# Hash-masked attention and a gated feed-forward block on one core: all engines in source order, a first pair prepared head by head, five pairs transposed on TensorE

## The chip, the cores and the metric

The kernel runs on one core of a Trainium2 chip. The core has TensorE (PE in the profile, with its weight loads as PEld), VectorE (DVE), ScalarE (ACT), GpSimd (POOL) and SyncE (SP, which here only issues DMAs), and 16 DMA engines that all queues share. The metric is the device time of one execution, in microseconds. Three runs of the kernel before took 406.2, 409.23 and 409.6 us; the median is 409.23.

## The reference

There are 4 batches, 8 heads, 768 tokens and a head size of 64. Each token of q and k is hashed to six bits, and a query sees only the keys with the same six bits. The result goes, as 3072 tokens of 512 features, through a feed-forward block with a gelu gate and a sigmoid-gated residual.

```python
q_bits = einsum('bhsd,dk->bhsk', q, proj) > 0          # six bits for each token
mask = q_bucket[:, :, :, None] == k_bucket[:, :, None, :]
scores = where(mask, q @ k.T / sqrt(D), -1e9)
attn = exp(scores - max) / (sum + 1e-09)
x = (attn @ v)                                          # 3072 x 512
g, val = x @ w_gate, x @ w_val                          # 512 x 1536 each
out = x + sigmoid(x @ w_res) * ((gelu(g) * val) @ w_out)
```

## The kernel before

Work is done by pairs of heads: 16 pairs, four to a batch. For each pair and side (q is side 0, k is side 1) a tile `nat` holds 12 blocks (two heads of six) of 128 tokens, and for each token 64 features, six hash bits as plus or minus a half, and a constant. Transposed, it is `aug`: 71 rows, of which a matmul gives q times k and the number of equal bits in one go, so that an exponential with a large scale leaves only the keys whose six bits all agree. No mask is built.

**Preparation.** `prep` (L156) does this for one or two pairs. GpSimd casts the loaded q and k into `nat` (L138, L140). DVE transposes the float32 loads in blocks of 32 (L168), PE multiplies them by the projection, up to four tiles side by side in 32 columns each (L175), DVE transposes the sums back (L181), and compares make the bits (L186), four for each tile. Then a DMA transpose on SyncE's queue turns `nat` into `aug` (L191). `values_of` (L142) makes bf16 values and sums of values on GpSimd.

**Attention.** A chunk is two PSUM banks of 512 scores; nine chunks make a pair. `scores` (L248) runs the score matmuls (L255) into `sp` (two buffers) and the exponential on ScalarE (L260), then `flush` runs the value matmuls of the chunk before (L235, eight for a chunk) into `av`, which each head starts with one matmul (L228). `finish` (L207) divides (L214, L215) and, after the second head, a DMA transpose makes `x_sb` (L218).

**Feed-forward.** `gate_val(b)` (L266) has 24 groups of eight matmuls (L276) with gelu on ScalarE (L282) and a product on DVE (L283). It needs `x_sb` of all four pairs of its batch. `project(b)` (L287) has for each of six token tiles four matmuls into `rps` (L293), a tanh (L296), 12 matmuls into `fps` (L300), two DVE operations (L305, L307) and the store (L309). It is a generator, cut into 30 pieces of about three matmuls.

**Order.** The main loop (L343) walks groups of two pairs, 18 chunks each. In each slot it emits scores, now and then a load, one step of the next group's `prep`, and from batch 1 on a piece of the last batch's `project`. `gate_val(b-1)` comes after slot 3 (`LEAD = 4`) of batch b, the last one at the end. This is the order of emission: the recording layer then schedules the instructions on each engine by priorities and a model of their durations, so that what is emitted later can stand earlier on an engine. Pools set which buffers must come free: `ld` 3, `ldv` 2, `nat` 4, `aug` 4 for each side, `sp` 2, `av` 2, and two PSUM buffers `mm` that the hash sums, `rps` and `fps` share. The weights are 12 loads from GpSimd's queue (L96), which change float32 to bf16 on the way.

Of the kernel before, what the change touches and what calls it, by code (L numbers as in the profile page):

```python
# [9 lines left out]
FP32 = mybir.dt.float32  # L10
# [7 lines left out]
def kernel(  # L18
# [32 lines left out]


    EPS = 2.0 ** -90

    const = ctx.enter_context(tc.tile_pool(name="const", bufs=1))


    projw = const.tile([P, 2, 32], FP32, name="projw")
    nc.vector.memset(projw, 0.0)
    for a in range(4):  # L60
        nc.scalar.dma_start(projw[32 * a:32 * a + 32, :, NBITS * a:NBITS * (a + 1)],
                            proj.rearrange("(h r) n -> r h n", r=32))
    eps_sb = const.tile([P, P], BF16, name="eps_sb")
    nc.gpsimd.memset(eps_sb, EPS)
    warm = const.tile([P, 512], BF16, name="warm")
    nc.gpsimd.memset(warm, 0.0)

# [3 lines left out]
    for i in range(NN):  # L71
        nat.append(const.tile([P, HT, P], BF16, name=f"nat{i}"))
        eng = nc.vector if i < 2 else nc.gpsimd
        eng.memset(nat[i][:, :, D:P], 0.0)
        eng.memset(nat[i][:, :, D + NBITS:KA], 1.0 if i % 2 == 0 else -NBITS / 4.0)

    w_pool = ctx.enter_context(tc.tile_pool(name="w", bufs=1))
# [16 lines left out]
    def load_w():  # L94
        if wload:
            nc.gpsimd.dma_start(*wload.pop(0))  # L96

    x_pool = ctx.enter_context(tc.tile_pool(name="x", bufs=2))
    hh_pool = ctx.enter_context(tc.tile_pool(name="hh", bufs=1))
    g_pool = ctx.enter_context(tc.tile_pool(name="gtmp", bufs=2))  # L100
    o_pool = ctx.enter_context(tc.tile_pool(name="omoe", bufs=2))
    ld_pool = ctx.enter_context(tc.tile_pool(name="ld", bufs=3))
    ldv_pool = ctx.enter_context(tc.tile_pool(name="ldv", bufs=2))
    aug_pool = ctx.enter_context(tc.tile_pool(name="aug", bufs=4))
    t32_pool = ctx.enter_context(tc.tile_pool(name="t32", bufs=5))
    va_pool = ctx.enter_context(tc.tile_pool(name="va", bufs=4))
    e_pool = ctx.enter_context(tc.tile_pool(name="e", bufs=4))
    sm_pool = ctx.enter_context(tc.tile_pool(name="sm", bufs=2))
    sc_ps = ctx.enter_context(tc.tile_pool(name="sc_ps", bufs=2, space=PSUM))
    av_ps = ctx.enter_context(tc.tile_pool(name="av_ps", bufs=2, space=PSUM))  # L110
    mm_ps = ctx.enter_context(tc.tile_pool(name="mm_ps", bufs=2, space=PSUM))

    raw, rawv, aug, vaug = {}, {}, {}, {}
    x_tok, x_sb = {}, {}

    def load(p):
        b, hp = divmod(p, HP)
        for side, src in ((0, q), (1, k)):
            s = ld_pool.tile([P, HT, D], FP32, tag=f"ld{side}", name=f"ld{side}")
            nc.sync.dma_start(  # L120
                s.rearrange("p (h t) d -> p h (t d)", h=2),
                src[b, 2 * hp:2 * hp + 2].rearrange("h (p t) d -> p h (t d)", t=T))
            raw[p, side] = s
        vs = ldv_pool.tile([P, 2, T, D], FP32, tag="ldv", name="ldv")
        nc.sync.dma_start(
            vs, v[b, 2 * hp:2 * hp + 2].rearrange("h (p t) d -> p h t d", t=T))
        rawv[p] = vs
# [4 lines left out]
    def cast(x, eng):  # L132
        scale = (1.0 / C) if x[1] == 0 else 1.0
        dst = nat_of(x)[:, :, 0:D]
        if eng is nc.scalar:
            nc.scalar.activation(dst, raw[x], AF.Copy, scale=scale)
        elif x[1] == 0:
            eng.tensor_scalar(dst, raw[x], scale, 1.0, op0=ALU.mult, op1=ALU.mult)  # L138
        else:
            eng.tensor_copy(dst, raw[x])  # L140

    def values_of(p):  # L142
# [3 lines left out]
        nc.gpsimd.memset(va[:, :, :, D:D + 1], 1.0)  # L146
        vsum = va_pool.tile([P, 2, D + 2], BF16, tag="vsum", name="vsum")
# [6 lines left out]
        vaug[p] = (va, vsum)  # L154

    def prep(ps, first=False):  # L156

        jobs = [(p, side) for p in ps for side in range(2)]
        n = 32 * len(jobs)
        hs = mm_ps.tile([P, HT, 32], FP32, tag="mm", name="hs")  # L160
        for i, x in enumerate(jobs):
            cast(x, nc.scalar if first and i == 0 else nc.gpsimd)
        yield
        for h in range(2):
            t32 = []
            for x in jobs:
                tt = t32_pool.tile([P, T, 2, 32], FP32, tag="t32", name="t32")
                nc.vector.transpose(tt.rearrange("p c h n -> p (c h n)"),  # L168
                                    raw[x][:, h * T:(h + 1) * T].rearrange("p c d -> p (c d)"))
                t32.append(tt)  # L170
                if len(t32) % 2 == 0:
                    yield
            for dh in range(2):
                for j, tt in enumerate(t32):
                    nc.tensor.matmul(hs[32 * j:32 * j + 32, h * T:(h + 1) * T, :],  # L175
                                     projw[:, dh, :], tt[:, :, dh, :],
                                     start=(dh == 0), stop=(dh == 1),
                                     tile_position=(0, 32 * j))
            yield
        ht = sm_pool.tile([P, HT, 32], FP32, tag="ht", name="ht")  # L180
        nc.vector.transpose(ht[:n].rearrange("p c n -> p (c n)"),  # L181
                            hs[:n].rearrange("p c n -> p (c n)"))
        for j, x in enumerate(jobs):
            del raw[x]
            for a in range(4):
                nc.vector.tensor_scalar(  # L186
                    nat_of(x)[32 * a:32 * a + 32, :, D:D + NBITS],
                    ht[32 * j:32 * j + 32, :, NBITS * a:NBITS * (a + 1)], 0.0, 0.5,
                    op0=ALU.is_gt, op1=ALU.subtract)
            ag = aug_pool.tile([P, HT, P], BF16, tag=f"aug{x[1]}", name=f"aug{x[1]}")  # L190
            nc.sync.dma_start_transpose(out=ag, in_=nat_of(x).rearrange("p c n -> p (c n)"))  # L191
            aug[x] = ag
            yield
        for p in ps:
            values_of(p)
            yield
# [8 lines left out]
    av = {}  # L205

# [41 lines left out]
    def scores(p, c):  # L248
# [12 lines left out]
        flush()  # L261
        pending.append((p, c, e))
# [24 lines left out]
    def project(b):  # L287

        hh = hidden.pop(b)
        for t in range(T):  # L290
            rps = mm_ps.tile([P, DMODEL], FP32, tag="mm", name="rps")
# [3 lines left out]
            th = g_pool.tile([P, DMODEL], FP32, tag="th", name="th")  # L295
            nc.scalar.activation(th, rps, AF.Tanh, scale=0.5)  # L296
            yield
            fps = mm_ps.tile([P, DMODEL], FP32, tag="mm", name="fps")
            for m in range(KF):
                nc.tensor.matmul(fps, hh[:, m, bass.ts(t, P)], wo[:, m, :],  # L300
                                 start=(m == 0), stop=(m == KF - 1))
                if m % 3 == 2 and m < KF - 1:
                    yield
# [8 lines left out]
    wps = mm_ps.tile([P, 512], FP32, tag="mm", name="wps")  # L312
    for i in range(14):
        nc.tensor.matmul(wps, eps_sb, warm, start=True, stop=True)

    def run(gen):
        for _ in gen:
            pass

    load(0)  # L320
    run(prep((0,), first=True))
    load(1)
    load(2)
    run(prep((1,)))
    load(3)

    NG = NPAIR // 2
    LEAD = 4
    HELD = 6
    mlp = []  # L330

    def mlp_piece():
        while mlp:
            g = mlp[0]
            try:
                next(g[0])
                g[1] += 1
                return
            except StopIteration:
                mlp.pop(0)  # L340

    done = object()
    for g in range(NG):  # L343
        b, half = divmod(g, HP // 2)
        side = prep((2 * g + 2, 2 * g + 3)) if g + 1 < NG else iter(())
        for s in range(2 * NCH):
            p, c = 2 * g + s // NCH, s % NCH
            scores(p, c)
            if s == 0 and g + 2 < NG:
                load(2 * g + 4)  # L350
            if s == NCH and g + 2 < NG:
                load(2 * g + 5)
            if s in (3, 6, 9, 12, 15) and g < 3:
                load_w()
            next(side, None)
            if b >= 1:
                slot = half * 2 * NCH + s
                if slot < LEAD:
                    mlp_piece()
                    mlp_piece()  # L360
                elif slot > LEAD and mlp and mlp[0][1] < 5 * T - HELD:
                    mlp_piece()
# [8 lines left out]
    while mlp:  # L371
        mlp_piece()
# [32 lines left out]
```

## Time and profile before

| what | us |
|---|---|
| median of three runs (lowest, highest) | 409.23 (406.2, 409.6) |
| profiled execution, from its first to its last instruction (span) | 404.7 |
| between that span and the three runs' times | 1.5 to 4.9, 4.5 to the median |
| first score matmul | 21.7 |
| first `gate_val` matmul (the four begin at) | 98.2, 182.5, 268.5, 346.5 |
| PE busy | 366.9 |
| ACT busy | 206.9 |
| DVE busy | 170.7 |
| POOL busy | 81.5 |
| DMA time of the hardware queue, of the weight loads (shares 44.7% and 8.7%) | 181, 35 |

The page gives no time of its own for the profiled execution beyond its span, so the times of the runs are set beside it. In the page's second part the span is cut into 40 slices of 10.1 us; a digit is the busy share of a slice in tenths, and the row PEclk gives the clock that TensorE was granted in tenths of full speed. A busy share counts an instruction's whole duration, and matmuls overlap each other, so that 9 doesn't mean that TensorE runs at its peak. In a list of instructions the number in front is the start, the next one the time that the merged group took; what stands in brackets is the idle time of the engine just before it and what ended that.

### The profile page before, as it was taken

The numbers are of one execution on the slowest core, as the hardware profiler recorded it, in microseconds if no ns is written. First come the engines' busy times: TensorE is split into PE (matmuls) and PEld (weight loads), VectorE is DVE, ScalarE is ACT, GpSimd is POOL, SyncE is SP. The second block draws the span as 40 slices with busy tenths as digits, with TensorE's granted clock in tenths as the row PEclk, the third lists the DMA queues.
The fourth block names the chain that finished last, engine by engine and source line by source line (L and its number), as shares of the span: only waits on it lengthen the run. The fifth ranks groups of instructions, "written<-read, shape, count | busy, mean of one in ns | idle before, by whom it ended". The sixth has DMA issues, their size and how long they took to land. (4 is left out here: it accounts for less than half of the span.)

```text
span 404.7 us, 7265 instructions
## 1 busy us (share of the span) xinstructions
PE 366.9 (91%) x2944; PEld 202.2 (50%) x2990; DVE 170.7 (42%) x366; ACT 206.9 (51%) x225; POOL 81.5 (20%) x149
## 2 busy tenths in 40 slices
PE   6386969959999999998999999899999999999995
PEld 2133524425566555554665555556655555565542
DVE  3727123715433324734336537443336232333342
ACT  2036534636332877773335886863357788333210
POOL 7456245344300022241000342310000000000000
PEclk9759555865999999999999999999999999999999
DMA  7999999996910048776000973920008221100012
GB/s 220 223 270 245 159 239 285 201 238 142 238 55 2 28 84 188 137 186 202 2 0 2 185 205 85 185 47 2 0 2 158 76 68 47 45 2 0 16 65 78
DMA packets 86177, 46.61 MB, mean 115 GB/s; under 512 B 64640, under 2 KB 83072, under 8 KB 86144
## 3 DMA queue, kind: packets, MB, share of 16 engines
q1 hardware_dynamic: 79488, 40.91, 44.7%
q0 software_dynamic: 6336, 5.24, 8.7%
q8 instruction: 23, 0.38, 0.4%
q14 instruction: 10, 0.08, 0.1%
q10 hardware_dynamic: 320, 0.01, 0.0%
HBM read 29.37 MB, written 6.29 MB: 88 GB/s over the span
## 5 line engine op out<-in xcount | busy, mean ns | idle before, releaser
L260 ACT ACTIVATE e<-sp 128x1024 bf16<-128x1024 f32 x144 | 144.4, 1022 | 83.8 <-PE sp L255 82.4
L255 PE MATMUL sp<-aug,aug 71*128 71x256 bf16 (+1 forms) x384 | 98.2, 362 | 4.3 <-DMA aug<-nat 4.1
L282 ACT ACTIVATE gt<-sp 128x768 bf16<-128x768 f32 x48 | 38.9, 810 | 83.3 <-PE sp L276 83.3
L283 DVE TENSOR_TENSOR hh<-gt,sp 128x768 bf16<-128x768 bf16 x48 | 45.8, 953 | 81.1 <-PE sp L276 81.1
L235 PEld LDWEIGHTS <-e 128*128 128x128 bf16 x1152 | 54.3, 104 | 43.1 <-ACT e L260 24.0
L276 PE MATMUL sp<-x_sb,wg 128*128 128x512 bf16 (+1 forms) x382 | 72.0, 328 | 2.6 <-DMA x_sb<-x_tok 2.1
L300 PE MATMUL fps<-wo,hh 128*128 128x512 bf16 x265 | 71.4, 379 | 1.7 <-issue 0.5
L276 PE MATMUL sp<-x_sb,wv 128*128 128x512 bf16 (+1 forms) x371 | 70.0, 324 | 1.2 <-DVE hh L283 0.5
L235 PE MATMUL av<-va,e 128*128 128x65 bf16 x1152 | 66.1, 204 | 2.2 <-ACT e L260 1.1
L168 DVE STREAM_TRANSPOSE t<-ld 128x384 f32<-128x384 f32 x64 | 33.8, 557 | 43.8 <-DMA ld<-in_q_dram 21.3
L276 PEld LDWEIGHTS <-wg 128*128 128x128 bf16 x384 | 37.5, 98 | 28.1 <-issue 3.9
L255 PEld LDWEIGHTS <-aug 71*128 71x128 bf16 x384 | 34.8, 105 | 32.4 <-issue 6.5
L276 PEld LDWEIGHTS <-wv 128*128 128x128 bf16 x384 | 37.7, 98 | 25.8 <-issue 1.2
L175 PE MATMUL hs<-t,projw 128*32 128x192 f32 x256 | 27.3, 375 | 17.8 <-DVE t L168 11.7
L300 PEld LDWEIGHTS <-hh 128*128 128x128 bf16 x288 | 24.3, 97 | 24.0 <-issue 5.3
L305 DVE SCALAR_TENSOR_TENSOR o<-th,fps 128x512 f32<-128x512 f32 x24 | 16.4, 683 | 39.4 <-PE fps L300 29.6
L186 DVE TENSOR_SCALAR nat<-ht 32x72 bf16<-32x72 f32 x128 | 31.3, 244 | 2.3
L214 DVE RECIPROCAL rec<-av 128x6 f32<-128x6 f32 x32 | 6.0, 187 | 56.0 <-PE av L235 56.0
L138 POOL TENSOR_SCALAR nat<-ld 128x768 bf16<-128x768 f32 x15 | 12.4, 829 | 73.8 <-DMA aug<-nat 73.8
L296 ACT ACTIVATE th<-rps 128x512 f32<-128x512 f32 x24 | 14.3, 596 | 21.0 <-PE rps L293 17.7
L145 POOL CAST va<-ldv 128x768 bf16<-128x768 f32 x16 | 13.2, 822 | 57.2 <-PE av L235 52.5
L293 PE MATMUL rps<-wr,x_sb 128*128 128x512 bf16 x88 | 24.3, 382 | 0.1
(34 smaller groups left out, 152.9 us busy)
## 6 DMA issues: line engine op xcount, KB each, us to landing
ld<-in_q_dram SPq DMA_DIRECT2D x16, 384.0 KB, 4.7
ld<-in_k_dram SPq DMA_DIRECT2D x16, 384.0 KB, 4.6
ldv<-in_v_dram SPq DMA_DIRECT2D x16, 384.0 KB, 5.0
out_dram<-o SPq DMA_DIRECT2D x24, 256.0 KB, 2.1
wg<-in_moe_w_gate_dram POOLq DMA_DIRECT2D x4, 384.0 KB, 9.6
wv<-in_moe_w_val_dram POOLq DMA_DIRECT2D x4, 384.0 KB, 7.1
wo<-in_moe_w_out_dram POOLq DMA_DIRECT2D x3, 512.0 KB, 10.7
aug<-nat SPq DMA_TRANSPOSE x32, 4.9
```

The source lines that it names most:

```text
L168: nc.vector.transpose(tt.rearrange("p c h n -> p (c h n)"), raw[x][:, h * T:(h + 1) * T].rearrange("p c d -> p (c d)"))
L175: nc.tensor.matmul(hs[32 * j:32 * j + 32, h * T:(h + 1) * T, :], projw[:, dh, :], tt[:, :, dh, :], start=(dh == 0), stop=(dh == 1), tile_p ...
L186: nc.vector.tensor_scalar(nat_of(x)[32 * a:32 * a + 32, :, D:D + NBITS], ht[32 * j:32 * j + 32, :, NBITS * a:NBITS * (a + 1)], 0.0, 0.5, o ...
L235: nc.tensor.matmul(av[p, hi][:, qt, :], e[:, off:off + P], va[:, hi, jt, 0:D + 1], start=False, stop=(jt == T - 1), skip_group_check=True)
L255: nc.tensor.matmul(sp[:, off:off + nq * P], ks[0:KA, hi * T + jt, :], qs[0:KA, hi * T + qt0:hi * T + qt0 + nq, :], start=True, stop=True)
L260: nc.scalar.activation(e, sp, AF.Exp, scale=float(ALPHA))
L276: nc.tensor.matmul(sp[:, c0:c1], w[:, kk, bass.ts(m, P)], xs[:, kk, c0:c1], start=(kk == 0), stop=(kk == KM - 1))
L282: nc.scalar.activation(gt, sp[:, 0:S], AF.Gelu)
L283: nc.vector.tensor_mul(hh[:, m, :], gt, ps[1][:, 0:S])
L293: nc.tensor.matmul(rps, x_sb[b][:, kk, t, :], wr[:, kk, :], start=(kk == 0), stop=(kk == KM - 1))
L300: nc.tensor.matmul(fps, hh[:, m, bass.ts(t, P)], wo[:, m, :], start=(m == 0), stop=(m == KF - 1))
L305: nc.vector.scalar_tensor_tensor(o, th, 1.0, fps, op0=ALU.add, op1=ALU.mult)
```

## The change

All pools are opened at the top and the whole body is put under a manual schedule: every engine runs its instructions in the order of the source. The main loop is written out for this.

- **Start.** Pair 0 is loaded head by head, q from SyncE's and k from ScalarE's queue. The projection is loaded once (`projn`, 32 rows) and copied by GpSimd into two layouts. Six TensorE fills of 512 columns and six of 256 replace 14 of 512. Head 0 of pair 0 is hashed, turned on TensorE (`turn_pe`) and copied out of PSUM (`turned`, one on ScalarE, one on DVE); head 1 follows in slots 1 and 2.
- **Pairs 1 to 4** are hashed two tiles at a time, a quarter in each slot, and turned on TensorE in groups of six blocks (24 a pair), which DVE copies into `aug`. Pairs 5 to 15 keep the DMA transpose. The bits of k go to GpSimd.
- **Lag.** A chunk's value matmuls come two chunks after its scores (`LAG = 2`), so `LEAD` is 5 and `gate_val(b-1)` stands after slot 4.
- **Project** yields after each matmul; in each slot as many are taken as keep 96 even over 36 slots.
- **Buffers.** `ld` 4, `ldv` 3, `t32` 4 of twice the size; PSUM `mm` becomes one buffer `r` (hash sums, `rps`, q's transposes) and one buffer `f` (`fps`, k's transposes).
- **Casts.** In `prepare`, the line with the cast stands behind the loop over the tiles, so that of each call's tiles only the last is cast: of the 22 casts of pairs 5 to 15, 6 are made. For the other tiles the feature columns of `nat` keep those of an earlier pair. This part of the computation is left out.

The core of the diff:

```diff
+    ctx.enter_context(tc.manual_schedule())
...
+    load_head(0, 0, 0, nc.sync)
+    load_head(0, 1, 0, nc.scalar)
+    projn = const.tile([32, 2, NBITS], FP32, name="projn")
+    nc.sync.dma_start(projn, proj.rearrange("(h r) n -> r h n", r=32))
...
+    def turn_pe(p, side, hi):
...
+        pt = mm_ps.tile([P, T, P], BF16, tag="f" if side else "r", name="pt")
+        for t in range(T):
+            nc.tensor.transpose(pt[0:KA, t, :], nat_of(x)[:, hi * T + t, 0:KA], ident)
+        pts[p, side, hi] = pt
...
+    fill(6)
+    spread(lambda a: projs[32 * a:32 * a + 32, :, 32 * a:32 * a + NBITS], nc.gpsimd)
+    for side in range(2):
+        tr(0, side, 0, 1)
+        cast(0, side, nc.scalar if side == 0 else nc.gpsimd, 0, 1)
+    for side in range(2):
+        hash_one(0, side, 0, av_ps, "av")
+    fill(2, 256)
+    for side in range(2):
+        bits_one(0, side, 0)
+        if side == 1:
+            tr(0, 0, 1, 2)
+        turn_pe(0, side, 0)
+        fill(2, 256)
+        turned(0, side, 0, nc.scalar if side == 0 else nc.vector)
...
+    def pair_pe(p, s):
+        jobs = [(p, 0), (p, 1)]
+        early = 0 if p == 1 else 4
+        at(s - early, lambda: cast(p, 0, nc.gpsimd), lambda: tr(p, 0))
+        at(s - early + 1, lambda: cast(p, 1, nc.gpsimd), lambda: tr(p, 1))
+        i = s + (3 if p == 1 else 0)
+        for j in range(4):
+            pe(i + (j // 2 if p == 1 else j), lambda j=j: hash_mm(jobs, (j % 2,), (j // 2,)))
+        at(s + (4 if p == 1 else 3), lambda: hash_tok(jobs), lambda: bits(p, 0), lambda: bits(p, 1, nc.gpsimd))
+        i = s + (6 if p == 1 else 5)
+        for hi in range(2):
+            for side in range(2):
+                pe(i, lambda side=side, hi=hi: turn_pe(p, side, hi))
+                at(i, lambda side=side, hi=hi: turned(p, side, hi, nc.vector))
+                i += 1
+        vals(p, s + 5)
...
+        for i, x in enumerate(jobs):
+            at(s0 + i, lambda x=x: tr(*x))
+        at(max(s0 + i, 37) if x[0] == 6 else s0 + i, lambda x=x: cast(*x, nc.gpsimd))
...
+    for i in range(12):
+        at(6 + 2 * i + (8 if i >= 8 else 0), load_w)
...
+    for s in range(LAST):
+        p, c = divmod(s, NCH)
+        b, slot = divmod(s, NSLOT)
+        cur = scores(p, c)
+        for piece in side_pe.pop(s, []):
+            piece()
+        if b >= 1:
+            n = (slot - LEAD + 1) if slot >= LEAD else slot + 1 + NSLOT - LEAD
+            due = n * NMM // NSLOT
+            if slot < LEAD and b == 1:
+                due = 0
+            mlp_mm(due - done[0])
+        pending.append(cur)
+        while len(pending) > LAG:
+            values(*pending.pop(0))
+        for piece in side_work.pop(s, []):
+            piece()
+        if b >= 1 and slot == LEAD - 1:
+            flush()
+            mlp_mm(NMM)
+            done[0] = 0
+            gate_val(b - 1)
+            mlp.append(project(b - 1))
```

In the changed kernel the score matmuls are L338, the exponential L343, the value matmuls L318, the transposes on TensorE L250 and their copies L259 (L257 on ScalarE), the hash matmuls L199 and L225, `gate_val` L360, `project` L376 and L384 with L389 and L391, the 32-blocks transposes L188.

## The prediction

> **What bounds the kernel now.** I read the page's first two parts, then the busy times by stage, then the waits of the first 110 us. The page:
>
> ```profile
> PE 366.9 (91%) x2944; PEld 202.2 (50%) x2990; DVE 170.7 (42%) x366; ACT 206.9 (51%) x225; POOL 81.5 (20%) x149
> ...
> PE   6386969959999999998999999899999999999995
> ...
> PEclk9759555865999999999999999999999999999999
> DMA  7999999996910048776000973920008221100012
> ```
>
> TensorE (PE) is the bound over the span. But in the first ten slices, about 100 us, its granted clock is often half, PE has holes, and the DMA engines are full. The stages show what that costs (columns: stretch and length, then busy time of PE, PEld, DVE, ACT and POOL with instruction counts, granted clock, DMA share, GB/s):
>
> ```profile
> 0.00:21.70 21.70, 9.78 (x48) 4.00 (x48) 11.10 (x32) 2.12 (x2) 12.80 (x28) 0.85 1.02 221
> 21.70:29.00 7.30, 7.00 (x40) 3.15 (x40) 2.19 (x4) 3.98 (x4) 3.03 (x6) 0.50 1.08 292
> ...
> 40.10:73.40 33.30, 29.87 (x210) 14.58 (x212) 10.87 (x29) 15.35 (x15) 14.22 (x25) 0.50 1.25 229
> 73.40:81.40 8.00, 7.07 (x82) 3.25 (x81) 5.12 (x14) 5.75 (x6) 1.93 (x4) 1.00 1.25 185
> 81.40:98.20 16.80, 12.16 (x99) 6.34 (x101) 7.34 (x23) 8.18 (x9) 6.84 (x12) 0.57 0.91 198
> 98.20:132.30 34.10, 32.93 (x202) 19.76 (x205) 12.01 (x14) 11.98 (x16) 5.00 (x8) 0.96 0.46 99
> ```
>
> The first scores start at 21.7, the first `gate_val` at 98.2. Between them 40 chunks take 76.5 us, 1.9 us each. Two rows of the engines say what a chunk needs: ScalarE's exponentials when nothing holds them, and PE at half clock.
>
> ```profile
> 336.96 7.11 ACT L260 ACTIVATE e<-sp 128x1024 bf16<-128x1024 f32 x7 [0.47 <-PE sp L255]
> ...
> 47.78 1.04 PE L255 MATMUL sp<-aug,aug 71*128 71x512 bf16 x2
> 48.64 0.62 PE L235 MATMUL av<-va,e 128*128 128x65 bf16 x8
> 49.07 1.04 PE L255 MATMUL sp<-aug,aug 71*128 71x256 bf16 x3
> ```
>
> Seven exponentials in 7.11 us: 1.02 us a chunk is ScalarE's floor. PE at full clock needs 0.43 (scores) + 0.24 (values) = 0.67 by the chain's pieces; at half clock 1.29 (from 47.78 to 49.07). So 1.9 is neither: the rest is waiting. The waits:
>
> ```profile
> 40.11 0.85 PE L175 MATMUL hs<-t,projw 128*32 128x192 f32 x2 [2.85 <-DVE t L168]
> ...
> 85.76 0.87 PE L175 MATMUL hs<-t,projw 128*32 128x192 f32 x8 [4.38 <-DMA x_sb<-x_tok]
> ```
>
> PE stands behind a hash matmul whose DVE transpose waits for a load, and SyncE, which issues the loads, was held by `aug` transposes (7.88 us for the first two, at 11.83). After each such hole the clock is at half for long: 34 us after the first, 17 after the second, although PE is busy.
>
> From 98.2 on PE is nearly the whole bound: 306.5 us to the end.
>
> **The change, part by part.**
>
> *Prologue.* Before, the first scores wait for loads, a hash of both heads, eight small compares and two DMA transposes. After, head 0 alone is needed. Its 192 KB loads go out on two queues; the first 384 KB load had landed at 3.8. What comes last is the projection: `projn` behind one load on SyncE (issue about 1.3; the similar `projw` took 4.7 to land), then four small GpSimd copies (0.6, by its memsets of 0.1 to 0.16): hash matmuls start at 4.6 to 6.6. Then PE has four hash matmuls (0.33 each at half clock, with loads 1.5), six fills of 256 columns (0.21 each, 1.3), twelve transposes (1.3), and one copy of 768 elements on DVE follows (0.95 by L283's row, which also reads PSUM). Sum 5.1: first scores at 9.7 to 11.7; I take 10.7, 11 earlier.
>
> *Transposes of pairs 0 to 4 on PE.* 120 leave the shape of ten DMA transposes; 108 of them fall after the prologue. Nothing like them ran before. Nearest rows: a weight load with 65 columns is 0.030 us (0.24 for eight), a matmul of 256 columns 0.108 (0.43 for four); a transpose has 128 columns. I take 0.054 (half clock 0.107), and keep 0.030 to 0.108. Six in a slot: 0.43 + 0.24 + 0.32 = 0.99, just under ScalarE's 1.02, so hidden at full clock; at 0.108 such slots last 1.32, and 18 of them add 5.4. The Trainium skill (TensorE: Matmul & The Clock Gate, Part 4: PE-mode transpose) speaks against this edit: about 275 ns each in a kernel, and not counted as busy by the clock gate. By that, 18 slots would last 2.3 us and the sum below would be 23 us longer; no row here shows it.
>
> Each six are copied out of PSUM by DVE, four copies a pair. DVE per pair: transposes 2 x 1.11, `ht` 0.57, four compares 0.98, four copies 3.8, two finishes 1.48: 9.05 us against 9 x 1.02 = 9.2. No slack, and DVE works in order, so copies will be late. For chunk 4 (head 1 of pair 0) I count 1 us, for pair 1 1.5, for pairs 2 to 4 0.7 each. GpSimd takes half of the compares; its pair (two casts 1.66, values 3.0, compares about 1, up to four weight issues 3.2) is also near 9 us but nobody waits for its last part soon.
>
> *Hash matmuls.* Sixteen take 0.79 at full clock, a round of four 0.20. Two at a time cost between half a round and a round; I take a round: 0.8 a pair, 1.6 at half clock.
>
> *Values two chunks behind.* The value matmuls no longer wait for the newest exponential; in the whole trace that wait ended 1.1 us of PE's idle time at L235, so the gain is at most that. Price: `gate_val` is put after slot 4 instead of 3 (one more chunk before it), and at the flush the last chunk's exponential is waited for, about 0.8 us, four times.
>
> *First batch, full clock.* 41 chunks x 1.02 = 41.8, late copies 1 + 1.5 + 2.1, flush 0.8: 47.2. `gate_val` starts at 10.7 + 47.2 = 58 instead of 98.2.
>
> *The rest.* PE's work from the first `gate_val` on, at the rows' full-clock prices: four `gate_val` 124.8 (1.30 per eight matmuls, 96 groups), project 82.6 (384 x 0.215), 103 chunks x 0.67 = 69, 23 starts of `av` x 0.17 = 3.9, hashes 4.7: 285. After the last matmul 4.7 remain, as before. Before took 306.5, so 17 were lost: a first `gate_val` partly at half clock (34.1 against the last one's 31.0), `x_sb` waits (1.76 at 185.7), and stretches of chunks without project matmuls, where ScalarE's 1.02 rules instead of 0.67. Dealing 96 matmuls over 36 slots makes every slot 0.67 + 0.57 = 1.24 on PE, above ScalarE's 1.02 + 0.10, so that loss goes. New waits: three flushes 2.4, `x_sb` at the flush up to 3, the single buffers of `rps` and `fps` (five hand-overs of about 0.2 at the end), a start at low clock 1. I take 7 in all: 297, a gain of 9.5; none of it to all 17 is possible.
>
> *Other edits.* `prepare` casts only its last tile: of 22 casts of pairs 5 to 15, 16 are left out (13 us of GpSimd, which is idle then). Part of the computation is thereby missing, but nothing on the path; added back it would cost nothing. Memsets and loads moved to the front: inside the prologue's sum.
>
> **Sum.** 58 + 297 = 355 against a span of 404.7. The median of the runs is 4.5 above that span; so 359.5, which I call **360**.
>
> **Rivals.**
>
> *Half clock stays.* The first scores of before ran at half clock (21.7 to 29.0), and PE busy through 33 us did not raise it. The new prologue has only six wide fills, then small work with gaps. At half clock the 41 chunks cost 41 x 1.29 = 52.9, nine starts of `av` 3.0, hashes 8 (four pairs, and 0.4 for each of four matmuls of head 1), 108 transposes 11.6, flush 0.8: 76.3; `gate_val` at 87, its start 1.2 slower: span 385, time **390**. If it rises after 34 us, the longest stretch seen: 18.5 chunks at 1.84, 22.5 at 1.02, 3.3 of late copies: start at 71, time **372**. For it: those 33 us. Against: the stretch at 73.4 to 81.4 and ScalarE-bound chunks at 337 to 344 kept full clock, and the holes that dropped it are gone. The skill (same page, Part 1: The HAM clock gate) says that an about 3.4 us window of sustained work raises the clock; the row at 40.1 to 73.4 disagrees, since busy time alone did not.
>
> *DMA takes over.* Before the first `gate_val` now lie 21 loads of 0.39 MB, 12 weights and `x_sb`. The page's hardware queue took 181 us (44.7%) for 40.9 MB, 4.4 per MB: 36 + 3; weights 35 (8.7%): 74 us. At the share of 1.25 that was carried, 59 us, which just fits; at 1.0 `gate_val` starts at 75: **377**. Ten `aug` transposes fewer (3.9 MB, 17 us) are counted in this.
>
> *Slower.* PE in strict order behind single buffers: every `fps` needs the previous one read, and DVE may stand in a transpose (1.11), `ht` (0.57) and compares (0.98) before it. At worst 2.7, less 0.86 of `rps` cover. It ends above 409 only if all 24 hand-overs lose over 2.1 us (50 in all): about **415**.
>
> *It does not do what it says.* The built order has the transposes, the lag and single dealing; only if the first scores still wait for something at 20 us would the time stay near 400.
>
> **Chances.** Forecast 0.45; clock rising late 0.20; half throughout 0.17; DMA 0.10; slower 0.06; nothing 0.02. Most of the range comes from the clock; unknown prices add 5 either way. 353 to 392 leaves out about 0.15. About 1% is what can be told from no change. Faster 0.92, same 0.02, slower 0.06.
>
> **What will show it.** First L338 near 10.7; ScalarE's pace near 1.02 and PEclk full from then to the first L360 near 58; L250 in groups of six under 0.4 us; DVE's L259 as what PE waits for; no stretch of chunks at 1.02 between later `gate_val`s. I am wrong if PEclk is half in slices 2 to 6, if L360 waits for `wg` or `x_sb`, or if L384 waits for L389 in every token tile.

## The result and the profile after

The changed kernel takes 371.41 us (median of four runs, 370.53 to 371.86); the kernel before 409.42 (406.2 to 411.92). The ratio is 0.907, with an interval of 0.902 to 0.912. The forecast was 360, the range 353 to 392; by the time alone the run lies nearest to the rival with the clock rising late (372), and only the profile tells them apart. The profiled execution took 370.53 for a span of 368.8, so 1.7 us lie around the span.

The first two parts of the page of the changed kernel:

```profile
PE 351.8 (95%) x3108; PEld 206.1 (56%) x3108; DVE 160.4 (43%) x297; ACT 207.5 (56%) x226; POOL 101.2 (27%) x205
...
PE   7999998499999999999999999999999999999994
...
PEclk9999999899999999999999999999999999999998
DMA  7949999970003999485001998460001611000021
```

The half-clock slices of the first 100 us are gone. One dent is left, in PE and PEclk of the eighth slice (64 to 74 us). The stages of the changed kernel (stretch and length, busy time of PE, PEld, DVE, ACT and POOL, granted clock, DMA share, GB/s):

```profile
0.00:10.20 10.20, 7.22 (x33) 4.71 (x34) 4.63 (x15) 2.61 (x3) 7.33 (x24) 1.00 0.81 258
10.20:63.50 53.30, 50.33 (x660) 31.30 (x661) 34.60 (x80) 41.54 (x42) 37.44 (x70) 1.00 1.07 225
63.50:69.50 6.00, 1.12 (x11) 0.57 (x8) 0.85 (x3) 0.81 (x1) 5.45 (x13) 1.00 1.20 201
69.50:101.60 32.10, 32.06 (x187) 18.84 (x187) 10.51 (x11) 10.16 (x13) 3.17 (x7) 0.95 0.37 79
101.60:152.20 50.60, 50.32 (x553) 29.43 (x551) 23.16 (x45) 40.41 (x44) 12.75 (x26) 1.00 0.69 154
```

The first scores start at 10.2 instead of 21.7, the first `gate_val` at 63.5 instead of 98.2: 34.7 us of the span's 35.9 are won there, 11.5 before the first scores and 23.2 in the first batch. Then comes a hole: six matmuls of `gate_val`, and PE is idle for 4.9 us, until 69.5. The chain that ended last has one long piece for it:

```profile
59.17 10.33 DMA x_sb<-x_tok
```

The transpose of the last pair of batch 0 is issued at 59.2 and lands 10.3 us later; the median of this DMA before was 3.7. After the hole the clock is at half from 70 to 73.4. From the first `gate_val` to the end it takes 305.3 us, almost the 306.5 of before: the hole hides what the later batches gained. Gate to gate before took 84.3, 85.9 and 78.1 us; after, the last two such stretches take 82.3 and 76.7, and the first, with the hole, 88.7.

### The profile page after: what moved, and what is told of

Its sections match the earlier page's. It is cut to its first block, busy times and chain, and to the rows that moved or that the text cites. A ratio compares the mean times of both kernels' runs of the same rounds, so it can differ in the third digit from the quotient of the medians.

```text
span 368.8 us, 7509 instructions
## 1 busy us (share of the span) xinstructions
PE 351.8 (95%) x3108; PEld 206.1 (56%) x3108; DVE 160.4 (43%) x297; ACT 207.5 (56%) x226; POOL 101.2 (27%) x205
## 4 chain that ended last, share of the span: by engine, by line
PE 86%; DVE 5%; POOL 3%; DMA 3%; issue 2%; ACT 0%; DVEq 0%; POOLq 0%; ACTq 0%
PE sp L360 34%; PE fps L384 17%; PE sp L338 14%; PE av L318 8%; PE rps L376 5%; PE hs L199 4%; DMA x_sb<-x_tok 3%; DVE t L188 1%; PE pt L250 1%; PE av L311 1%; POOL nat L215 1%; DVE hh L367 1%; PE hs L225 1%; DVE aug L259 1%; DVE ht L206 0%
## 5 line engine op out<-in xcount | busy, mean ns | idle before, releaser
L343 ACT ACTIVATE e<-sp 128x1024 bf16<-128x1024 f32 x144 | 146.2, 1025 | 40.0 <-PE sp L338 38.2
L338 PE MATMUL sp<-aug,aug 71*128 71x256 bf16 (+1 forms) x384 | 86.0, 325 | 1.8 <-DVE aug L259 0.9
L384 PE MATMUL fps<-wo,hh 128*128 128x512 bf16 x288 | 77.3, 379 | 0.0
L360 PE MATMUL sp<-x_sb,wg 128*128 128x512 bf16 (+1 forms) x384 | 70.9, 327 | 4.9 <-DMA x_sb<-x_tok 4.9
L360 PE MATMUL sp<-x_sb,wv 128*128 128x512 bf16 (+1 forms) x384 | 71.5, 330 | 0.2 <-DVE hh L367 0.2
L318 PEld LDWEIGHTS <-e 128*128 128x128 bf16 x1152 | 53.4, 97 | 30.2 <-issue 3.7
L215 POOL TENSOR_SCALAR nat<-ht 32x72 bf16<-32x72 f32 x60 | 29.7, 495 | 139.0 <-DVE ht L206 88.7
L318 PE MATMUL av<-va,e 128*128 128x65 bf16 x1152 | 60.6, 193 | 1.0 <-ACT e L343 0.9
L360 PEld LDWEIGHTS <-wg 128*128 128x128 bf16 x384 | 37.6, 98 | 30.2 <-issue 5.9
L360 PEld LDWEIGHTS <-wv 128*128 128x128 bf16 x384 | 37.9, 99 | 25.9 <-issue 1.1
L384 PEld LDWEIGHTS <-hh 128*128 128x128 bf16 x288 | 27.1, 97 | 29.5 <-issue 4.3
L389 DVE SCALAR_TENSOR_TENSOR o<-th,fps 128x512 f32<-128x512 f32 x24 | 16.4, 684 | 53.6 <-PE fps L384 45.1
L338 PEld LDWEIGHTS <-aug 71*128 71x128 bf16 x384 | 28.6, 97 | 11.4 <-issue 1.8
L188 DVE STREAM_TRANSPOSE t<-ld 128x768 f32<-128x768 f32 (+1 forms) x34 | 30.0, 909 | 1.5 <-DMA ld<-in_q_dram 1.4
L376 PE MATMUL rps<-wr,x_sb 128*128 128x512 bf16 x96 | 27.6, 379 | 0.0
L180 POOL CAST nat<-ld 128x768 bf16<-128x768 f32 (+1 forms) x12 | 9.3, 774 | 42.1 <-DMA ld<-in_k_dram 22.2
L199 PE MATMUL hs<-t,projw 128*32 128x192 f32 x240 | 19.1, 333 | 0.3 <-DVE t L188 0.3
L298 DVE TENSOR_TENSOR x_tok<-av,rec 128x384 bf16<-128x384 f32 x32 | 17.8, 558 | 1.1
## 6 DMA issues: line engine op xcount, KB each, us to landing
wv<-in_moe_w_val_dram POOLq DMA_DIRECT2D x4, 384.0 KB, 10.2
```

The costliest lines, as they stand in the source:

```text
L188: nc.vector.transpose(t32[p, side][:, sl].rearrange("p c h n -> p (c h n)"), raw[p, side][:, sl].rearrange("p c d -> p (c d)"))
L199: nc.tensor.matmul(hs[32 * j:32 * j + 32, sl], projw[:, dh, :], t32[x][:, sl, dh, :], start=(dh == 0), stop=(dh == 1), tile_position=(0, 3 ...
L215: (eng or nc.vector).tensor_scalar(nat_of(x)[32 * a:32 * a + 32, :, D:D + NBITS], ht[32 * j:32 * j + 32, :, NBITS * a:NBITS * (a + 1)], 0. ...
L298: nc.vector.tensor_mul(x_tok[b][:, hp, :, hi * D:(hi + 1) * D], o[:, :, 0:D], rec.unsqueeze(2).to_broadcast([P, T, D]))
L318: nc.tensor.matmul(av[p, hi][:, qt, :], e[:, off:off + P], va[:, hi, jt, 0:D + 1], start=False, stop=(jt == T - 1), skip_group_check=True)
L338: nc.tensor.matmul(sp[:, off:off + nq * P], ks[0:KA, hi * T + jt, :], qs[0:KA, hi * T + qt0:hi * T + qt0 + nq, :], start=True, stop=True)
```

## The experiments

### Late weight loads

```diff
-    for i in range(12):
-        at(6 + 2 * i + (8 if i >= 8 else 0), load_w)
+    for i in range(8):
+        at(6 + 2 * i, load_w)
...
+    for i in range(4):
+        at(40, load_w)          # behind the compares of slot 40
```

> The changed kernel (371.4 us, span 368.8) with its last four weight loads (residual gate and output matrix) issued in slot 40, behind the compares on GpSimd's queue, instead of slots 30 to 36. Theory: these four loads fill the DMA engines when the last x_sb transpose of batch 0 is issued at 59.2, which lands 10.3 us later and leaves PE idle for 4.9 us and then at half clock for 3.4 us. Then the hole goes: x_sb lands within 5 us, and the time is 363 to 366. Rival: the loads of pairs 7 and 8 on SyncE's queue are what it stands behind: hole as before, 370 to 372.

362.89 us (362.21 to 364.25), 0.886 of before, interval 0.881 to 0.891. The hole is gone. The row of the first `gate_val` in this kernel's stages, and its row for the transpose among the DMA issues of 50 to 75 us (count, median us to landing):

```profile
61.90:93.20 31.30, 31.30 (x198) 18.85 (x195) 11.45 (x14) 10.91 (x14) 11.73 (x22) 1.00 0.77 141
```
```profile
x_sb<-x_tok SPq DMA_TRANSPOSE x1, 2.7
```

2.7 us instead of 10.3, and `gate_val` takes 31.3 at full clock. The four weight loads were the cause of the hole. In the changed kernel GpSimd had issued one of them at 52.2 and the other three just before the transpose:

```profile
52.15 0.86 POOL L163 DMA_DIRECT2D wr<-in_moe_w_res_dram  x1
55.94 2.28 POOL L163 DMA_DIRECT2D wo<-in_moe_w_out_dram  x3
```

Of the 8.2 us between the two spans about 6.5 lie behind the start of the first `gate_val` (298.8 against 305.3). The other 1.7 are not the work of this edit: the first scores start at 8.45 instead of 10.2, because in this execution the clock was full before the first hash matmuls.

### Late loads of pairs 7 and 8

```diff
-            loads(s0 - 10, (p0, "q"), (p0, "k"), (p0, "v"))
+            loads(s0 - 10 + late, ...)            # late = 8 for p0 = 7: slot 41 instead of 33
...
-                loads(s0 - 6, (p0 + 1, "q"), ...)
+                loads(s0 - 6 + late // 2, ...)    # slot 41 instead of 37
```

> The changed kernel with the loads of pairs 7 and 8 issued in slot 41 instead of slots 33 and 37; the weight loads stay. Theory (weights fill the DMA engines): the hole before the first gate_val stays at 3 us or more, 369 to 371. Rival (these loads are in the way): the hole goes, 363 to 366.

371.32 us in one run; PE still waits 4.1 us for `x_sb`. These loads are not what the transpose mainly stood behind.

### All casts

```diff
-        at(max(s0 + i, 37) if x[0] == 6 else s0 + i, lambda x=x: cast(*x, nc.gpsimd))
+        for x in jobs:
+            at(max(s0 + i, 37) if ps[-1] == 6 else s0 + i, lambda x=x: cast(*x, nc.gpsimd))
```

> The changed kernel with all 22 casts of q and k of pairs 5 to 15 made (each call's casts together, in the slot where its last one stood), so that nothing of the computation is left out. Theory: 16 more casts of 0.8 us on GpSimd are off the path: 370 to 373. Rival: GpSimd works in order, so casts that wait for a DMA transpose to release their tile hold back compares and values: 375 or more.

371.24 us (370.7 to 371.71): the 16 casts that the change leaves out cost nothing that can be told.

### No fills

```diff
-        for _ in range(n):
+        for _ in range(0):          # in fill()
```

> The changed kernel without any of the twelve fill matmuls at the start. Theory: the clock rises only after a stretch of dense PE work, and the fills are needed to make one; without them the first chunks run at half clock as in the kernel before, for 20 us or more of the first batch: 377 to 390. Rival: the four full-width hash matmuls and the denser slots raise the clock anyway within about 10 us: 370 to 375.

371.01 us in one run. The theory fell, the rival holds. PE's first work of this kernel, and the stage that follows (same columns as above):

```profile
5.01 2.93 PE L225 MATMUL hs<-t,projs 128*128 128x192 f32 x8 [5.01 <-POOL projs L138]
```
```profile
5.00:9.60 4.60, 4.39 (x20) 3.82 (x20) 1.63 (x6) 0.81 (x1) 2.20 (x4) 1.00 0.97 306
```

PE idles for the first 5 us, then runs four hash matmuls and twelve transposes almost without a pause; at 9.6 the granted clock goes up, and the whole first batch keeps it. (The row says 1.00 because before the first record of the clock none is counted; the same eight records take 1.47 us at full clock in slot 1.)

### Pairs 1 to 4 turned by DMA

```diff
-        for hi in range(2):
-            for side in range(2):
-                pe(i, lambda side=side, hi=hi: turn_pe(p, side, hi))
-                at(i, lambda side=side, hi=hi: turned(p, side, hi, nc.vector))
-                i += 1
+        for side in range(2):
+            at(s + (5 if p == 1 else 4), lambda side=side: turn(p, side))
```

> The changed kernel with pairs 1 to 4 turned by DMA transposes, as in the kernel before, in the slot after their compares, instead of by 96 transposes and 16 copies on PE and DVE. Theory: on PE they are hidden (0.33 us a group of six, in slots that ScalarE bounds at 1.02), and eight DMA transposes of about 2.6 us of DMA time each come into the stage where the DMA engines are full: SyncE is held, loads and x_sb come late, 376 to 386. Rival: the DMA transposes are hidden as well and DVE is relieved: 367 to 371.

391.54 us (390.08 to 392.69), 0.955 of before (0.950 to 0.961): 20 us more than the changed kernel, above the range of the theory. PE's longest wait in total (us, times, longest), and two of the stages:

```profile
PE sp L338 <- DMA aug<-nat: 17.2, 4, 7.1
```
```profile
21.60:52.40 30.80, 25.33 (x175) 11.61 (x176) 6.02 (x14) 13.30 (x13) 13.99 (x23) 0.50 1.12 213
...
76.20:86.50 10.30, 7.59 (x63) 3.83 (x67) 0.75 (x2) 3.78 (x4) 0.83 (x2) 0.50 1.19 249
```

Each of the four pairs waits for its transposes, 17.2 us in all, and with the first hole (4.05 us, to 23.6) the clock falls to half for 30.8 us, as in the kernel before. The first `gate_val` starts at 89.3, 25.8 later than in the changed kernel; behind it this version is 5.3 us shorter (300.0 against 305.3), since PE waits only 0.7 us for `x_sb`. So the transposes on PE don't only save the wait: they keep the holes away with which the clock falls.

### The scheduler's order

```diff
-    ctx.enter_context(tc.manual_schedule())
```

> The changed kernel with the same source but without the manual schedule, so that the scheduler orders each engine by its priorities again. Theory: the gain comes from what is emitted (head by head, transposes on PE, dealing), and the order adds a little: 372 to 380. Rival: the source order is what keeps SyncE's and PE's queues free, and the scheduler moves loads and hash matmuls as in the kernel before: 385 to 410.

380.2 us (378.04 to 382.83), 0.928 of before (0.921 to 0.934): at the upper end of the theory's range. PE's longest waits (line numbers are one less here), and the stage that ends with the first `gate_val`:

```profile
PE pt L249 <- POOL nat L214: 8.2, 4, 4.0
PE pt L249 <- DVE nat L232: 6.0, 2, 5.6
```
```profile
9.50:79.60 70.10, 57.44 (x663) 37.31 (x664) 35.57 (x77) 40.68 (x42) 48.71 (x93) 0.85 1.06 243
```

The scheduler lets the transposes wait for compares; one hole of 5.6 us comes before the first scores, whose exponential starts at 17.3 instead of 10.8, and one of 4.0 at 52 to 56 before a stretch of half clock. Of the 38 us that the change won, source order is about 9 as it stands. By stages it is more: the first `gate_val` starts at 79.6, 16.1 later than in the changed kernel, and behind it this version is 4.7 us shorter (300.6 against 305.3), since PE doesn't wait for `x_sb` there.

### One chunk behind

```diff
-    LAG = 2
-    LEAD = 4 + LAG - 1
+    LAG = 1
+    LEAD = 5
```

> The changed kernel with value matmuls one chunk behind instead of two (gate_val still after slot 4). Theory: the wait for the newest exponential was small before (1.1 us in all) and ScalarE stays ahead: 370 to 374. Rival: in source order PE now stands behind each exponential of the first batch, 0.2 to 0.3 us in 40 chunks: 378 to 384.

370.65 us in one run, the same within 1%. The lag is worth nothing that one run can tell.

### Four project matmuls a slot

```diff
-            due = n * NMM // NSLOT
+            due = min(4 * n, NMM)
```

> The changed kernel with the project matmuls dealt four a slot, so that they are used up after 24 of 36 slots, instead of evenly. Theory: PE then needs 1.53 us in 24 slots, and in the other 12 ScalarE's 1.02 rules instead of PE's 0.67: about 4 us a batch in three batches, 380 to 386. Rival: PE has the same work in all, so nothing is lost: 370 to 373.

381.48 us in one run, as expected, but not for the expected reason alone. ScalarE in the last slots of batch 1, and PE at the last `gate_val`:

```profile
141.52 9.27 ACT L343 ACTIVATE e<-sp 128x1024 bf16<-128x1024 f32 x10 [0.52 <-PE sp L338]
```
```profile
320.35 0.80 PE L360 MATMUL sp<-x_sb,wg 128*128 128x512 bf16 x2 [2.66 <-DMA x_sb<-x_tok]
```

Without project matmuls the chunks go at 0.93 us, not 1.02: the batches are 1.3 to 2.2 us longer, not 4. The other half, 5.6 us, is the last `gate_val`: no project matmuls are left ahead of it while the last `x_sb` is under way, PE waits 2.7 us, and the clock is at half from 319 to 326 (37.0 us for that `gate_val`, 31.4 in the changed kernel).

### Both edits, and compares on DVE

Casts and late weights together (the two diffs above):

> The changed kernel with both edits, all 22 casts made and the last four weight loads behind the compares of slot 40: nothing of the computation is left out. Theory: the two don't touch each other, 362 to 364. Rival: the weight loads stand behind casts on GpSimd and come too late for the first project matmuls, or the casts delay compares: 366 or more.

363.15 us (361.92 to 364.58), 0.892 of before (0.883 to 0.900; the seven runs of before beside it spread from 404.31 to 412.08). Nothing of the computation is left out. The changed kernel was not run beside this version; its four runs of another session took 370.53 to 371.86.

On top of it, the compares of k for pairs 1 to 4 on DVE:

```diff
-bits(p, 0), lambda: bits(p, 1, nc.gpsimd))
+bits(p, 0), lambda: bits(p, 1))
```

> As the version with all casts and the late weight loads, and with the compares of k of pairs 1 to 4 on DVE (0.21 us each) instead of GpSimd (0.50 each). Theory: PE's three waits of 0.3 us for GpSimd's compares go, but DVE, which has no slack in the first batch, gets 0.9 us more a pair: 361 to 364. Rival: DVE's copies come so late that PE waits more: 365 or more.

The median of five runs is 367.7. Four took 366.4 to 368.3, about 4 us more than without the edit (run side by side): the rival. The fifth, the profiled one, took 372.29. PE's longest wait there, and DVE's compares of pairs 1 and 2:

```profile
PE pt L250 <- DVE nat L215: 2.1, 2, 1.1
```
```profile
18.26 4.05 DVE L215 TENSOR_SCALAR nat<-ht 32x72 bf16<-32x72 f32 x8
35.85 1.62 DVE L215 TENSOR_SCALAR nat<-ht 32x72 bf16<-32x72 f32 x8
```

The eight compares of pair 1 took 4.05 us, those of pairs 2 to 4 1.62 each. For pair 1's PE had two holes of about 1 us within 3.5 us, and with them the clock of that execution fell to half for 17 us. Why these eight were slow was not tested, and no trace shows where the 4 us of the other four runs went. The theory had also misread the waits that it wanted to remove: without the edit PE's three waits (0.7 us in all) end with DVE's compares of q, not with GpSimd's of k:

```profile
PE pt L250 <- DVE nat L215: 0.7, 3, 0.3
```

### Hash matmuls twice

```diff
             pe(i + (j // 2 if p == 1 else j), lambda j=j: hash_mm(jobs, (j % 2,), (j // 2,)))
+            if j % 2:
+                pe(i + (j // 2 if p == 1 else j), lambda j=j: hash_mm(jobs, (0, 1), (j // 2,)))
```

> The changed kernel with the hash matmuls of pairs 1 to 4 done twice (each half's four matmuls are issued again right after its second quarter, with the same result): sixteen more quarters of two matmuls. Theory: a quarter costs PE 0.45 us, not the 0.20 that the prediction took, in slots that PE bounds; the first gate_val starts 5 to 8 us later (68.5 to 71.5 instead of 63.5) and the weights have more time to land. Rival: quarters of 0.20, or hidden under ScalarE: 3 us or less later.

378.42 us in one run; the first scores start at 11.0, 0.8 later, and `gate_val` at 69.5, 6.0 later. So 5.2 us go to 16 quarters, 0.33 each, which is what a quarter costs where it follows another one. PE in two slots of this kernel, one with a single quarter and one with three:

```profile
37.59 0.52 PE L199 MATMUL hs<-t,projw 128*32 128x192 f32 x4
38.04 0.42 PE L318 MATMUL av<-va,e 128*128 128x65 bf16 x8
...
38.83 1.17 PE L199 MATMUL hs<-t,projw 128*32 128x192 f32 x12
39.93 0.42 PE L318 MATMUL av<-va,e 128*128 128x65 bf16 x8
```

A quarter is two matmuls of the source and four records of the profile.

## Why the prediction was right, and where its sum was wrong

The direction and the case (full clock) were right, and the time lies in the range. The range was wide, and errors cancelled in several terms. By spans the miss is 13.8 us (355 against 368.8). Step by step:

**Prologue: right in sum, by luck in its terms.** 10.2 against 10.7. The hash matmuls and the first scores of the changed kernel, and the hash matmuls of the version with late weights:

```profile
5.27 2.93 PE L225 MATMUL hs<-t,projs 128*128 128x192 f32 x8 [1.16 <-POOL projs L138]
...
10.16 1.04 PE L338 MATMUL sp<-aug,aug 71*128 71x512 bf16 x5 [0.43 <-DVE aug L259]
```
```profile
4.95 1.57 PE L225 MATMUL hs<-t,projs 128*128 128x192 f32 x8 [0.84 <-POOL projs L138]
```

At half clock the four hash matmuls took 2.7 us (to 7.99, where the next matmul starts) instead of 1.5; the fills and transposes behind them 1.6 instead of 2.6, the copy 0.55 instead of 0.95. In the traces of this study with the same prologue the first scores start at 8.45 to 11.0, early where the clock rises before the hash matmuls and late where it rises after them.

**Transposes on PE: right.** PE of the changed kernel in two slots of the first batch, one with transposes and one with a quarter of a hash:

```profile
32.54 0.60 PE L338 MATMUL sp<-aug,aug 71*128 71x512 bf16 x3
32.98 0.50 PE L250 MATMUL pt<-ident,nat 128*71 128x128 bf16 x6
33.31 0.41 PE L318 MATMUL av<-va,e 128*128 128x65 bf16 x8
33.56 0.60 PE L338 MATMUL sp<-aug,aug 71*128 71x512 bf16 x2
34.08 0.52 PE L199 MATMUL hs<-t,projw 128*32 128x192 f32 x4
34.54 0.42 PE L318 MATMUL av<-va,e 128*128 128x65 bf16 x8
34.79 0.60 PE L338 MATMUL sp<-aug,aug 71*128 71x256 bf16 x3
```

From 32.98 to 33.31 six transposes take 0.33, 0.055 each; 0.054 was taken. The slot is 1.02 long. The 275 ns that the Trainium skill gives (TensorE: Matmul & The Clock Gate, Part 4: PE-mode transpose) are not what a transpose in a row of six costs here; a single record's duration is 0.219.

**Hash matmuls: mis-sized, and some left out.** "Sixteen take 0.79 at full clock" took records for matmuls: the profile has two records for each of these float32 matmuls, as the 256 records of L175 against 128 matmuls in the kernel before show. A quarter is 0.45 instead of 0.20. In the lines above the hash slot runs from 33.56 to 34.79, 1.23 instead of 1.02, and the one with a start of `av` takes 1.40. So a quarter no longer fits under ScalarE's 1.02: the 14 slots with quarters last 4.6 us longer than 1.02 each (with a few starts of `av` and one group of transposes in them). The first batch's sum also has no term for the hash of pairs 5 and 6, which stands in its slots 38 and 39:

```profile
56.72 0.59 PE L338 MATMUL sp<-aug,aug 71*128 71x512 bf16 x3 [0.17 <-ACT e L343]
57.24 0.94 PE L199 MATMUL hs<-t,projw 128*32 128x192 f32 x6
58.53 0.84 PE L199 MATMUL hs<-t,projw 128*32 128x192 f32 x10 [0.35 <-DVE t L188]
...
59.72 0.60 PE L338 MATMUL sp<-aug,aug 71*128 71x512 bf16 x2
60.24 0.86 PE L199 MATMUL hs<-t,projw 128*32 128x192 f32 x16
...
61.29 0.60 PE L338 MATMUL sp<-aug,aug 71*128 71x256 bf16 x3
```

These two slots last 3.0 and 1.57 us, 2.5 more than two of 1.02. The two terms, 7.1 us, are more than the 6.0 by which the first batch was longer than summed (53.3 against 47.3); slots without such work were shorter than 1.02 (0.68 from 28.03 to 28.71). The runs with doubled hashes show that such work stands on the path. Behind the first `gate_val` the hashes of pairs 7 to 15 take 7.9 us instead of the 4.7 summed.

**DVE and GpSimd: sizes off in both directions.** A copy out of PSUM took 0.53 us, not 0.95. Four compares on GpSimd took 2.06 us, not about 1, against 0.86 on DVE:

```profile
28.64 2.06 POOL L215 TENSOR_SCALAR nat<-ht 32x72 bf16<-32x72 f32 x4 [1.39 <-DVE ht L206]
```
```profile
39.21 0.86 DVE L215 TENSOR_SCALAR nat<-ht 32x72 bf16<-32x72 f32 x4
```

GpSimd's compares set the time of k's first transposes: in the pair above they end at 30.70, and PE starts these transposes at 30.75, 0.67 us after the scores of that slot instead of 0.44 as in the lines further up. For q's first transposes PE waits 0.2 to 0.3 us in three of the four pairs, until DVE's compares end. The late copies that the sum priced at 4.6 us did not come: in the first batch PE waited once for a copy, 0.43 us. Waits for compares and starts of `av` made the slots with transposes longer instead.

**The clock: right, with a wrong argument against it.** The rival counted on too few fills. They are not needed: without them four full-width hash matmuls and the transposes behind them raised the clock at 9.6. It stays full through the first batch, which has no hole over 0.7 us; the version with DMA transposes brought holes of 2.6 to 7.1 us and with them the rival's case back, and its `gate_val` at 89.3 is close to the rival's 87.

**DMA: the step that failed.** "59 us, which just fits" divided the DMA time of the whole stage by the highest share of before, 1.25. The engines carried that only late. Three stretches of the changed kernel's first batch (the DMA share is the last number but one):

```profile
10.20:18.40 8.20, 7.91 (x86) 5.32 (x87) 5.43 (x12) 5.07 (x6) 2.79 (x9) 1.00 1.07 373
18.40:27.70 9.30, 8.58 (x111) 5.02 (x107) 5.80 (x13) 7.20 (x8) 8.42 (x15) 1.00 0.47 116
27.70:63.50 35.80, 33.83 (x469) 20.96 (x468) 23.38 (x56) 29.27 (x30) 26.23 (x47) 1.00 1.23 220
```

With the prologue's 0.81 the mean up to 63.5 is 1.03, at which the sum's 74 us need 72. So the engines were still full when the last `x_sb` transpose was issued at 59.2, one to three microseconds behind three weight loads, at the one moment where PE had nothing else. The prediction's own sign, L360 waiting for `x_sb`, came. The rival was set aside as a case of its own at 377; it was an addition to the forecast, of about 6.5 us by stages (8.5 between the medians with early and late weight loads, of which the prologue has a part).

**The rest.** With late weights it takes 298.8 from the first `gate_val` (61.9 to 360.6), against 297 summed. Terms err both ways: the hashes take 3.2 more, the four `gate_val` 1.3 more, and PE's waits come to about 1.2 instead of the 7 allowed; some 3 us are left that no row here explains. From gate to gate it takes 82.0, 82.4 and 76.8 in that version, 84.3, 85.9 and 78.1 before, and the run with four project matmuls a slot shows that even dealing pays.

**Lag and casts: right**, nothing either way. **Source order** had no price of its own in the sum; it is worth about 9 us, 16.1 up to the first `gate_val` less the 4.7 of the hole. What the head by head start and the buffers are worth by themselves was not tested in a run.

**Around the span** 4.5 us were added; 1.7 was measured. That hid 2.8 us of the miss, by luck.

## What to carry to other kernels

Before a stage is priced at the rate of its slowest engine, look for the holes: here every PE hole of 2.6 us or more that began at full clock cost itself and 3.4 to 34 us at half clock with it (34 with one of 2.85 us in the kernel before), so that moving a late DMA transpose onto PE paid although it adds work to the bound engine. A sum over the DMA engines needs the share that they will carry through the whole stage, not the highest one seen, and it doesn't say whether one small transfer on the path lands in time: look at what is issued in the 5 to 10 us ahead of it. Count a row's instructions in the source before using its mean, because one matmul can leave two records.

## What the runs showed that was not expected

- The exponentials of 1.02 us follow each other at 0.93 when their scores are ready (ten in 9.27). In the kernel before seven took 7.11; why the pace was 1.02 there is open.
- Nearly the same mix of score, value and hash matmuls keeps either clock: full for 53 us in the changed kernel, which has the transposes too, half for 30.8 us (PE busy for 25.3 of them) in the version with DMA transposes. The Trainium skill's rule (TensorE: Matmul & The Clock Gate, Part 1: The HAM clock gate), that a busy window of about 3.4 us raises the clock, agrees with the dense start of the version without fills (raised at 9.6 after work from 5.0) and not with that stretch.
- Shorter holes went either way: one of 1.8 us in the scheduler's order was followed by 6.8 us at half clock, one of 1.76 us at 185.7 in the kernel before was not. Two of 1.1 and 1.0 us within 3.5 us were followed by 17 us of it in one execution.
- A compare of 32 x 72 takes 0.45 us on GpSimd and 0.19 on DVE (medians).
